# Batch 0's first products halved straight from PSUM by ScalarE and VectorE, with fewer state DMAs and a new order of the opening

## The chip, the cores and the metric

One core of a Trainium2 chip. The metric is the device time of one execution in microseconds, the median of three runs. The engines are TensorE (PE: matmuls; PEld: its weight loads), VectorE (DVE), ScalarE (ACT), GpSimd (POOL) and SyncE (SP), which issues most DMAs.

## What is computed

x is (8, 8, 512, 64), that is batches, heads, rows, width; state is (8, 8, 32, 64); w_ch1 is 512 x 2048, w_ch2 2048 x 512. Each batch is a two-way attention and then a feed-forward layer over the concatenated rows:

```python
s  = x @ state.T / 8;   a  = softmax(s);   xread = a @ state      # 512 rows per head
s2 = state @ x.T / 8;   a2 = softmax(s2);  sread = a2 @ x         # 32 rows per head
y  = concat([xread, sread]).transpose(0, 2, 1, 3).reshape(8, 544, 512)
yn = (y - mean) / sqrt(var + 1e-6) * g_ln
out = y + relu(yn @ w_ch1) @ w_ch2                                # (8, 544, 512), float32
```

## The kernel before

Every float32 product is made of three float16 products: both factors are split into a high half (the value rounded to float16) and a low half (the value minus its high half), and high x high, high x low and low x high are summed. A split so costs two instructions: ScalarE writes the high half, and another engine, mostly VectorE, subtracts it and writes the low half.

The first layer is not computed from xread. Per batch and unit u (the 2048 hidden columns are four units of 512) `state_products` (L656) multiplies the state with w1 (L662), which gives a small `matrix`; the hidden columns then are the softmax numerators `ea` times `matrix`: L705 in batch 0, L798 in the batches from 1 on. Behind that come relu, split, and the product with `w2h`, the split second weights: L719 in batch 0, L856 in the others, where the second layer goes by Strassen's scheme with the sums of weight blocks `sums`. The scores of a batch are made from transposes of x and state (`xT`, `sT`, two xT transposes per batch by DMA; L400), the second softmax's product is L474.

In the opening the weights arrive as raw words (`raw`, `sums` as buffers), are put together (`w_t`), w1 is weighted with g_ln and freed of its column means (L589, `acc`), the largest size is found (L598), and `w1c` and `w2h` are the scaled and split results, 128 x 2048 each per unit. ScalarE writes their high halves, VectorE the low ones. `x` is batch data split to float16, `x_f` the loaded one; `s_j`, `s_r` are loads of state, `sh`, `sk` its splits; `eb` numerators of the second softmax, `ef`, `ts` steps on the way to `ea`; `of_weights`, `uoq`, `hs` scales; `mv`, `rs`, `rf`, `of_unit` the layer norm's statistics; `part` the scaled second product of batch 0 on its way out; `z`, `sread` the second attention's result.

Batch 0's hidden tiles are made by `first_products` (L694 to L713): four units of four tiles of 128 x 512, each in one PSUM bank of the pool `acc` (four banks). `hidden` (L683) then takes three instructions: ScalarE's relu copies the bank into a strip in SBUF (three strips in turn), ScalarE copies the strip to the high half, GpSimd subtracts the high half from the strip. With `engine=nc.vector` nobody calls it before the change. In the batches from 1 on hidden tiles are split by other code, `strassen_hidden`.

Nothing of the order is left to a scheduler: every step is a closure made by `do` (so the profile shows L194 for all but matmuls), steps are gathered in streams (0 the gain, 1 the attention of batch 0, 2 to 5 the first weights, 6 state products, 7 first products, 8 to 11 the second weights, 17 to 20 the second products of batch 0 by unit, 25 and 26 attention and state products of batch 1, and so on, about 20 per batch), and the table `PLAN` names stream and step in the order of issue. Each engine runs its own instructions in that order, and a waiting instruction holds up all behind it on its engine; DMAs wait in the queue of the engine that issues them.

Of the kernel before, what the change touches and what calls it, by code (L numbers as in the profile page):

```python
# [10 lines left out]
F16 = mybir.dt.float16  # L11
# [157 lines left out]
WARM = 0  # L169


class Later:
# [36 lines left out]
def moe_attention(ctx: ExitStack, tc: tile.TileContext, x, state, g_ln, w1, w2, out):  # L209
# [27 lines left out]
    def rows(name):  # L237
        return block(8, "rows", 2, name)
# [742 lines left out]
```

## Time and profile before

| | us |
|---|---|
| median of 3 runs | 640.9 (640.69 to 643.12) |
| the profiled execution | 642.75 |
| its span | 641.0 |
| mean granted clock of TensorE | 0.971 |

The span is what the trace covers; 1.75 us of the execution lie around it. Shares and rows of the profile belong to the profiled execution. In rows of groups stand line, engine, operation, output <- inputs, their shapes, the count, then busy time and the mean ns of one, and behind the last bar the idle time of the engine ahead of them with what ended it. In the chain and the timeline stand the start and the length in us. DMA issues on the sync queue are marked SPq.

### The profile page before, as it was taken

How to read it: one execution, taken by the hardware profiler on the slowest of the kernel's cores; microseconds unless marked ns; L12 is line 12 of the kernel's file. 1: busy time of each engine (PE TensorE's matmuls, PEld its weight loads, DVE VectorE, ACT ScalarE, POOL GpSimd, SP SyncE). 2: the span in 40 equal slices, each digit the busy share in tenths (PEclk: the TensorE clock that was granted, in tenths of full speed). 3: DMA queues.
4: the chain of work that ended last, by engine and by line, in shares of the span. 5: the costliest groups of instructions: out<-in, count | busy, mean ns of one | idle time of the engine just before them, and what ended most of it. 6: DMA issues, size and time to landing. Idle time of an engine off the chain costs nothing.

```text
span 641.0 us, 15125 instructions
## 1 busy us (share of the span) xinstructions
PE 603.9 (94%) x6218; PEld 480.6 (75%) x6220; DVE 478.3 (75%) x954; ACT 369.1 (58%) x651; POOL 249.7 (39%) x213
## 2 busy tenths in 40 slices
PE   2769899899999999999999999999999999999996
PEld 1226556457978888888888778888888889898885
DVE  4999799778896779786976897677866878466344
ACT  4488999777564755644646553755465454344331
POOL 0013754387662324442532334234432443234122
PEclk9956799899999999999999999999999999999998
DMA  8985439523624243233631323304330404401002
GB/s 304 298 310 187 137 95 153 121 50 75 147 38 132 60 100 72 76 82 69 166 78 43 72 73 79 106 20 89 90 94 1 108 3 84 139 15 34 11 24 68
DMA packets 89382, 62.60 MB, mean 98 GB/s; under 512 B 67616, under 2 KB 81440, under 8 KB 88864
## 3 DMA queue, kind: packets, MB, share of 16 engines
q1 hardware_dynamic: 86512, 57.66, 34.3%
q0 software_dynamic: 864, 3.15, 2.6%
q8 instruction: 49, 0.80, 0.5%
q10 hardware_dynamic: 1936, 0.82, 0.5%
q14 instruction: 21, 0.17, 0.1%
HBM read 28.05 MB, written 9.44 MB: 58 GB/s over the span
## 4 chain that ended last, share of the span: by engine, by line
PE 83%; DVE 7%; ACT 5%; DMA 3%; issue 2%; ACTq 0%; SPq 0%; DVEq 0%
PE acc L856 42%; PE half L798 23%; PE acc L719 3%; PE half L808 3%; PE banks L662 3%; PE acc L705 3%; DVE w_t L194 2%; PE banks L474 2%; DMA xT<-x 1%; DMA sums<-in_moe_w_ch_dram 1%; PE banks L505 1%; PE banks L400 1%; PE acc L589 1%; ACT sums L194 1%; ACT raw L194 1%
## 5 line engine op out<-in xcount | busy, mean ns | idle before, releaser
L856 PEld LDWEIGHTS <-xs 128*128 128x128 f16 x2520 | 243.7, 98 | 36.4 <-issue 6.8
L194 POOL TENSOR_TENSOR xs<-rs,xs 128x512 f16<-128x512 f32 x120 | 139.8, 1179 | 234.9 <-ACT xs L194 154.3
L856 PE MATMUL acc<-w2h,xs 128*128 128x256 f16 x1440 | 181.1, 273 | 0.0
L798 PE MATMUL half<-ea,matrix 128*128 128x256 f16 x1344 | 160.9, 273 | 1.3 <-DVE rs L194 0.8
L798 PEld LDWEIGHTS <-matrix 128*128 128x128 f16 x1344 | 129.6, 98 | 21.6 <-issue 3.4
L856 PE MATMUL acc<-sums,xs 128*128 128x256 f16 x1080 | 141.8, 273 | 0.0
L194 DVE SCALAR_TENSOR_TENSOR rs<-half,rs 128x256 f32<-128x256 f32 x224 | 90.2, 416 | 48.5 <-ACT rs L194 25.4
L194 ACT ACTIVATE xs<-rs 128x512 f16<-128x512 f32 (+1 forms) x128 | 76.3, 618 | 55.0 <-DVE rs L194 47.7
L194 ACT ACTIVATE xs<-half 128x256 f16<-128x256 f32 (+1 forms) x112 | 52.9, 486 | 54.0 <-DVE rs L194 25.8
L194 DVE SCALAR_TENSOR_TENSOR xs<-half,xs 128x256 f16<-128x256 f32 (+1 forms) x112 | 60.9, 549 | 14.1 <-ACT xs L194 13.9
L194 ACT ACTIVATE rs<-half 128x256 f32<-128x256 f32 x56 | 21.2, 379 | 63.5 <-PE half L798 61.8
L719 PE MATMUL acc<-w2h,hid 128*128 128x512 f16 x192 | 43.0, 379 | 0.4 <-ACT part L194 0.4
L194 DVE SCALAR_TENSOR_TENSOR matrix<-banks,hs,matrix 128x1024 f16<-128x1024 f32 x28 | 35.6, 1273 | 9.6 <-ACT matrix L194 9.6
L194 DVE TENSOR_TENSOR strip<-acc,strip 128x256 f32<-128x256 f32 (+1 forms) x61 | 33.2, 544 | 6.5 <-ACT strip L194 3.0
L194 POOL TENSOR_TENSOR ts<-ts,mA 128x1024 f32<-128x1024 f32 (+1 forms) x8 | 14.4, 1805 | 53.8 <-DVE mA L194 44.0
L194 ACT ACTIVATE matrix<-banks,hs 128x1024 f16<-128x1024 f32 x28 | 31.0, 1109 | 7.1 <-PE banks L662 6.5
L719 PEld LDWEIGHTS <-hid 128*128 128x128 f16 x192 | 18.4, 98 | 22.2 <-issue 1.2
L705 PE MATMUL acc<-ea,matrix 128*128 128x256 f16 x192 | 29.0, 316 | 1.0 <-ACT xr L194 0.5
L194 POOL TENSOR_TENSOR hid<-strip,hid 128x512 f16<-128x512 f32 x16 | 21.3, 1342 | 19.5 <-ACT hid L194 19.5
L194 DVE SCALAR_TENSOR_TENSOR x<-x_f,x_s,x 128x512 f16<-128x512 f32 x32 | 25.3, 814 | 4.2 <-ACT x L194 4.1
L705 PEld LDWEIGHTS <-matrix 128*128 128x128 f16 x192 | 21.3, 113 | 8.4 <-issue 1.8
L589 PE MATMUL acc<-w_t,gm 128*128 128x512 f32 x32 | 19.3, 755 | 8.2 <-DVE w_t L194 8.2
(154 smaller groups left out, 752.1 us busy)
## 6 DMA issues: line engine op xcount, KB each, us to landing
raw<-in_moe_w_ch_dram SPq DMA_DIRECT2D x10, 1024.0 KB, 6.8
out_dram<-xr SPq DMA_DIRECT2D x16, 512.0 KB, 3.4
x_f<-in_x_dram SPq DMA_DIRECT2D x14, 512.0 KB, 5.5
sums<-in_moe_w_ch_dram SPq DMA_DIRECT2D x6, 1024.0 KB, 7.7
ek<-ea SPq DMA_DIRECT2D x56, 64.0 KB, 2.0
ek<-ek SPq DMA_DIRECT2D x7, 512.0 KB, 4.3
xr<-part POOLq DMA_DIRECT2D x6, 512.0 KB, 4.6
s_r<-in_state_dram SPq DMA_DIRECT2D x28, 64.0 KB, 2.4
```

The lines of the kernel that those rows point to most:

```text
L194: return lambda: f(*map(now, args), **{k: now(v) for k, v in kw.items()})
L400: nc.tensor.matmul(ps[32 * j:32 * j + 32, g, w * s:w * s + w], lhsT=sT[D * g:D * g + D, a, 32 * j:32 * j + 32], rhs=xT[D * g:D * g + D, k: ...
L474: nc.tensor.matmul(ps_z[:, j], lhsT=x16[:, a, i], rhs=ebT[:, k, :, c, 32 * j:32 * j + 32], start=c == 0 and n == 0, stop=c == C - 1 and n ...
L505: nc.tensor.matmul(px[:, c, D * h:D * h + D], lhsT=ek[:, h % 2, h // 2, (2 * t + c) * P:(2 * t + c + 1) * P], rhs=sk[:, h], start=True, st ...
L589: nc.tensor.matmul(ps, lhsT=gm[:, k:k + 1].broadcast_to([P, P]), rhs=t4[:, k], start=k == 0, stop=k == 3)
L662: nc.tensor.matmul((ps0, ps1)[g][32 * j:32 * j + 32], lhsT=sT[D * g:D * g + D, a, 32 * j:32 * j + 32], rhs=w[D * g:D * g + D, i, j], start ...
L705: nc.tensor.matmul(o[:, 256 * f:256 * f + 256], lhsT=m[:, g, i, P * (q + f):P * (q + f) + P], rhs=ea[:, s, k, g], start=f == 0 and g == 0 ...
L719: nc.tensor.matmul(po, lhsT=hid[:, i, q, c * P:(c + 1) * P], rhs=w[:, j, q], start=first and q == 0 and n == 0, stop=last and q == 3 and n ...
L798: nc.tensor.matmul(ps[:, 256 * q:256 * q + 256], lhsT=m[:, h, i, P * (2 * k + q):P * (2 * k + q) + P], rhs=ea[:, 0, j, h, 256 * g:256 * g ...
L808: nc.tensor.matmul(ps[:, 256 * q:256 * q + 256].rearrange("p (t n) -> p t n", t=2), lhsT=w[:, i, j, fs], rhs=xsT[:, :, 4 * a + j], start=q ...
L856: nc.tensor.matmul(po[o], lhsT=y[:, n, i, o] if o < 2 else x[:, o - 2, n, i], rhs=v[j], start=u == 0 and n == 0 and k == 0 and o in (2, 1, ...
```

## The change

Three pieces of code and the order.

`hidden` gets a direct form for `engine=nc.vector`: ScalarE writes the high half from PSUM, VectorE reads the bank again and writes max(p, 0) minus the high half. All 16 tiles of `first_products` use it, so stream 7 has 48 steps instead of 64.

```diff
     def hidden(ps, scale, hi, lo, n, engine=nc.vector):
+        if engine is nc.vector:
+            p = ps.rearrange("p (f t) -> p f t", f=n)
+            yield do(nc.scalar.activation, hi, p, AF.Relu)
+            yield do(nc.vector.scalar_tensor_tensor, lo, p, 0.0, hi, ALU.max, ALU.subtract)
+            return
         strips[0] += 1
...
-                    yield from hidden(ps, 1.0, *(h[:, i, q:q + 2, 256 * s:256 * s + 256] for i in range(2)), 2, nc.gpsimd)
+                    yield from hidden(ps, 1.0, *(h[:, i, q:q + 2, 256 * s:256 * s + 256] for i in range(2)), 2, nc.vector if DIRECT[4 * u + 2 * s + q // 2] else nc.gpsimd)
```

`DIRECT` is a tuple of 16 ones. The loads of `s_j` of the batches from 1 on are two DMAs instead of four, the store of a batch's `sread` rows is one instead of four, and `ek` is laid out with its two middle indices exchanged (as many DMAs as before):

```diff
+        if b == 0:
+            for j in range(4):
+                yield do(engines[j // 2].dma_start, out=sj[32 * j:32 * j + 32], in_=state[b, 2 * j:2 * j + 2].rearrange("g n d -> n g d"))
+        else:
+            for g in range(G):
+                yield do(nc.sync.dma_start, out=sj[:, g], in_=state[b].rearrange("(j g) n d -> g j n d", g=G)[g])
...
-            ek = rows("ek").bitcast(F16).rearrange("p (g j t) -> p g j t", g=G, j=4)
+            ek = rows("ek").bitcast(F16).rearrange("p (j g t) -> p j g t", g=G, j=4)
...
-        for j in range(4):
-            yield do(nc.sync.dma_start, out=sv[NS * b:NS * b + NS, j], in_=sread[32 * j:32 * j + 32])
+        yield do(nc.sync.dma_start, out=sread_rows[NS * b:NS * b + NS].rearrange("n (j e) -> j n e", j=4),
+                 in_=sread.rearrange("p g d -> p (g d)"))
```

`PLAN` is written anew up to the last second products of batch 1; behind that it is the same apart from the numbers of steps. A line of it, the beginning, before and after:

```diff
-    "0:0 1:1 1:6-7 1:5 1:0 1:2 1:9 1:3 0:2 1:4 0:5 1:12 1:8 1:10-11 1:13-15 0:3 1:16-19 4:0 4:2-3 4:1 2:0 1:79 1:26 "
+    "0:0 0:2 1:1 1:9 1:7 1:3 1:0 1:4 1:2 0:5-6 1:6 1:5 4:0 1:8 1:11 4:1 1:12 1:10 1:13-15 2:0 0:3 1:16 4:2-3 2:1 "
```

With the change all lines of the kernel move a little: `do` is L192 instead of L194, L705 becomes L711, L719 L725, L798 L804, L856 L862, L662 L663, L400 L402 and L589 L590.

On the engines the new order shows at three places. The names `of_weights`, `uoq` and `is` are scales of weights, `mv` and `s` statistics of row blocks, `x_t`, `x_m`, `x_i`, `x_s` the way to the scale of a batch's x.

The first is VectorE ahead of the low half of `w2h` of unit 0, the last row; the matmuls of L719 hang on that. Before:

```order
L194 SCALAR_TENSOR_TENSOR w1c<-w_t,of_weights,w1c 128x2048
L194 TENSOR_SCALAR uoq<-of_weights,is_298 128x1
L194 RECIPROCAL of_weights<-of_weights 128x1
L194 TENSOR_REDUCE x_t<-banks 2x1
L194 TENSOR_REDUCE of_weights<-acc 128x1
L194 TENSOR_SCALAR of_weights<-of_weights 128x1
L194 BN_AGGR mv<-s_736 128x2
L194 BN_STATS s_813<-xr 128x6
L194 SCALAR_TENSOR_TENSOR w2h<-w_t,of_weights,w2h 128x2048
```

And after:

```order
L192 SCALAR_TENSOR_TENSOR hid<-acc,hid 128x2x256
L192 TENSOR_SCALAR x_m<-banks 128x2
L192 BN_AGGR mv<-s_584 128x2
L192 SCALAR_TENSOR_TENSOR hid<-acc,hid 128x2x256
L192 TENSOR_SCALAR x_i<-x_m 128x2
L192 TENSOR_REDUCE of_weights<-acc 1x1
L192 SCALAR_TENSOR_TENSOR w1c<-w_t,of_weights,w1c 128x2048
L192 RECIPROCAL x_s<-x_i 128x2
L192 TENSOR_SCALAR of_weights<-acc 128x1
L192 SCALAR_TENSOR_TENSOR w2h<-w_t,of_weights,w2h 128x2048
```

Two of the new low halves of hidden tiles (`hid<-acc,hid`) have come in, four more stand further ahead; a BN_STATS of 128x512 and the reduce of 128x512 (`of_weights<-acc 128x1`) have moved behind.

The second place is the sync queue with the transposes of batch 0. Before:

```order
L194 DMA s_j<-in_state_dram 32x2x64
L575 DMA sums<-in_moe_w_ch_dram 128x2x1024 x2
L575 DMA raw<-in_moe_w_ch_dram 128x2x1024 x4
L575 DMA sums<-in_moe_w_ch_dram 128x2x1024
L194 DMA_TRANSPOSE xT<-x_108 128x16x128
L194 DMA_TRANSPOSE sT_198<-sh 128x2x128
L194 DMA_TRANSPOSE xT<-x_108 128x16x128
```

And after:

```order
L192 DMA s_j<-in_state_dram 32x2x64 x2
L576 DMA sums<-in_moe_w_ch_dram 128x2x1024 x2
L576 DMA raw<-in_moe_w_ch_dram 128x2x1024 x4
L192 DMA_TRANSPOSE xT<-x_108 128x16x128
L192 DMA_TRANSPOSE sT_167<-sh 128x2x128
L192 DMA_TRANSPOSE xT<-x_108 128x16x128
L576 DMA sums<-in_moe_w_ch_dram 128x2x1024
```

The third load into `sums` has moved behind the three transposes.

The third place is VectorE ahead of the low half of `ea` of batch 1, the last row; the first L798 hangs on that. Before:

```order
L194 SCALAR_TENSOR_TENSOR sums<-t_582,of_weights,sums 128x512
L194 TENSOR_REDUCE dA<-ts 128x32
L194 TENSOR_SCALAR dA<-dA 128x32
L194 RECIPROCAL dA<-dA 128x32
L194 SCALAR_TENSOR_TENSOR matrix<-banks,hs,matrix 128x2x512
L194 STREAM_TRANSPOSE ef<-ts 128x1024
L194 SCALAR_TENSOR_TENSOR xr<-acc,of_unit,xr 128x512
L194 SCALAR_TENSOR_TENSOR ea<-ef,ea 128x1024
```

And after:

```order
L192 SCALAR_TENSOR_TENSOR hid<-acc,hid 128x2x256
L192 SCALAR_TENSOR_TENSOR sums<-t_587,of_weights,sums 128x512
L192 TENSOR_REDUCE x_am<-s_j 128x1
L192 SCALAR_TENSOR_TENSOR sums<-t_654,of_weights,sums 128x512
L192 TENSOR_REDUCE dA<-ts 128x32
L192 TENSOR_SCALAR dA<-dA 128x32
L192 RECIPROCAL dA<-dA 128x32
L192 SCALAR_TENSOR_TENSOR sums<-t_587,of_weights,sums 128x512
L192 SCALAR_TENSOR_TENSOR xr<-acc,of_unit,xr 128x512
L192 STREAM_TRANSPOSE ef<-ts 128x1024
L192 SCALAR_TENSOR_TENSOR matrix<-banks,hs,matrix 128x2x512
L192 SCALAR_TENSOR_TENSOR ea<-ef,ea 128x1024
```

The fifteenth of the 16 new low halves (first row) now stands shortly ahead of ea's, the sixteenth behind it.

On TensorE, one group of 24 L662 of batch 0 (a unit's state products) stands behind the first matmuls of L719 instead of ahead of them, and 12 matmuls of L719 more stand behind the first L798 of batch 1; otherwise the matmuls between these two are as many as before.

More of the change, by code (lines that the diff above doesn't have):

```diff
@@ L41 @@
 PLAN = (
[127 rows of a table removed]
[124 rows of a table added]
 WARM = 0
+DIRECT = (1, 1, 1, 1, 1, 1, 1, 1, 1, 1, 1, 1, 1, 1, 1, 1)
 class Later:
@@ L295, in load_batch @@
                 yield do(engines[hh].dma_start, out=o, in_=i[:, :, 2 * hh:2 * hh + 2] if b == 0 else i)
-        for j in range(4):
-            yield do(engines[j // 2].dma_start, out=sj[32 * j:32 * j + 32], in_=state[b, 2 * j:2 * j + 2].rearrange("g n d -> n g d"))
+        if b == 0:
[4 more added lines that the diff above has]
+                yield do(nc.sync.dma_start, out=sj[:, g], in_=state[b].rearrange("(j g) n d -> g j n d", g=G)[g])
         for r in range(4 if b > 0 else 0):
@@ L488, in attention @@
         if b > 0:
-            ek = rows("ek").bitcast(F16).rearrange("p (g j t) -> p g j t", g=G, j=4)
+            ek = rows("ek").bitcast(F16).rearrange("p (j g t) -> p j g t", g=G, j=4)
             for i in range(2):
                 for j in range(4):
-                    yield do(nc.sync.dma_start, out=ek[32 * i:32 * i + 32, :, j], in_=ea[32 * j:32 * j + 32, 0, i])
+                    yield do(nc.sync.dma_start, out=ek[32 * i:32 * i + 32, j], in_=ea[32 * j:32 * j + 32, 0, i])
             yield do(nc.sync.dma_start, out=ek[64:128], in_=ek[0:64])
-        sv = sread_rows.rearrange("n (j g d) -> n j g d", g=G, j=4)
-        for j in range(4):
-            yield do(nc.sync.dma_start, out=sv[NS * b:NS * b + NS, j], in_=sread[32 * j:32 * j + 32])
+        yield do(nc.sync.dma_start, out=sread_rows[NS * b:NS * b + NS].rearrange("n (j e) -> j n e", j=4),
+                 in_=sread.rearrange("p g d -> p (g d)"))
         ux = column("ux")
@@ L505, in mix @@
                         nc.tensor.matmul(px[:, c, D * h:D * h + D],
-                                         lhsT=ek[:, h % 2, h // 2, (2 * t + c) * P:(2 * t + c + 1) * P],
+                                         lhsT=ek[:, h // 2, h % 2, (2 * t + c) * P:(2 * t + c + 1) * P],
                                          rhs=sk[:, h], start=True, stop=True, skip_group_check=True)
@@ L941, in moe_attention @@
     streams += [list(s) for s in products(B)]
-    warm = half()
     def warmth():
         for _ in range(WARM):
-            yield do(nc.tensor.matmul, warm, lhsT=ones, rhs=ones.unsqueeze(1).broadcast_to([P, 4, P]), start=True, stop=True)
+            yield do(nc.tensor.matmul, half(), lhsT=ones, rhs=ones.unsqueeze(1).broadcast_to([P, 4, P]), start=True, stop=True)
     streams.append(list(warmth()))
```

249 rows, old and new, of the table PLAN are left out of this document.

## The prediction

> **What bounds the kernel now.** I read the page first: the engines' shares, and TensorE's row and clock in the 40 slices of 16.0 us.
>
> ```profile
> span 641.0 us, 15125 instructions
> PE 603.9 (94%) x6218; PEld 480.6 (75%) x6220; DVE 478.3 (75%) x954; ACT 369.1 (58%) x651; POOL 249.7 (39%) x213
> PE   2769899899999999999999999999999999999996
> PEclk9956799899999999999999999999999999999998
> ```
>
> TensorE is the bound in all but the first eight slices, and what is weak behind the start is the eighth slice (112 to 128 us, clock 0.8). So I asked what TensorE waited for, over the whole span and then from 75 us on.
>
> ```profile
> PE banks L194 <- DVE x_am L194: 8.7, 1, 8.7
> PE acc L589 <- DVE w_t L194: 8.2, 5, 3.5
> ...
> PE banks L400 <- DMA xT<-x: 2.1, 1, 2.1
> PE half L798 <- DVE rs L194: 0.8, 1, 0.8
> PE half L798 <- DVE xs L194: 0.6, 1, 0.6
> PE acc L719 <- ACT part L194: 0.4, 1, 0.4
> ```
>
> The last four are all there is after 75 us. So a change of the opening can gain by an earlier start of L719 (batch 0's second products, from where TensorE always has work) and by the removal of the 2.1 us wait with what follows from it. The chain of waits shows what follows.
>
> ```profile
> 106.31 8.84 DMA xT<-x
> 115.19 1.48 PE banks L400 x17
> 116.67 2.31 PE acc L705 x12
> 118.98 5.18 PE acc L719 x24
> 124.16 1.31 PE acc L705 x12
> 125.47 0.77 PE banks L662 x24
> ```
>
> Behind the wait, L400's 24 matmuls of 64x512 take 1.48 us where L662's 24 of the same shape take 0.77, and L705 takes 2.31 where it takes 1.31 later: TensorE runs at about half rate for 3.8 us, which costs 0.71 + 1.00 = 1.71 us.
>
> Then the timeline, for the instructions that release TensorE at three places.
>
> ```profile
> 78.86 2.57 DVE L194 SCALAR_TENSOR_TENSOR w2h<-w_t,of_weights,w2h 128x2048 f16<-128x2048 f32 x1 [0.62 <-ACT w2h L194]
> 81.20 8.00 PE L719 MATMUL acc<-w2h,hid 128*128 128x512 f16 x36
> 104.06 0.73 DVE L194 SCALAR_TENSOR_TENSOR x<-x_f,x_s,x 128x512 f16<-128x512 f32 x1
> 138.03 2.33 DVE L194 SCALAR_TENSOR_TENSOR ea<-ef,ea 128x1024 f16<-128x1024 f32 x1 [0.55 <-ACT ea L194]
> 141.52 0.71 PE L798 MATMUL half<-ea,matrix 128*128 128x256 f16 x5
> ```
>
> L719 starts as VectorE's low half of w2h for unit 0 ends (81.4). L400 of batch 1 starts at 115.19, when xT has landed, 10.4 us after the last low half of batch 1's x (104.06 + 0.73 = 104.79). L798, the first product of batch 1, needs ea's low half, which ends at 140.36; TensorE came only at 141.52, so that one was ready in time. How busy the engines are between these points (columns: stretch, length, then busy time and count of PE, PEld, DVE, ACT, POOL):
>
> ```profile
> 12.30:81.50 69.20, 53.72 (x418) 29.09 (x421) 63.91 (x112) 54.42 (x76) 20.44 (x13) 0.78 0.74 241
> 81.50:92.30 10.80, 10.80 (x58) 5.44 (x57) 9.95 (x25) 10.80 (x14) 4.97 (x4) 1.00 0.28 99
> 92.30:140.40 48.10, 45.53 (x390) 24.71 (x389) 40.58 (x57) 38.83 (x59) 26.64 (x22) 0.96 0.60 114
> ```
>
> VectorE is busy 63.91 + 9.95 + 40.58 = 114.44 of 128.10 us, so 13.66 us of it are idle, 5.29 of them before L719. That is the room into which the change puts work.
>
> **The change part by part.** *Direct halving.* These rows are the groups of 40 to 150 us and, for VectorE, two neighbours of the timeline.
>
> ```profile
> L194 ACT ACTIVATE strip<-acc 128x512 f32<-128x512 f32 x16 | 9.4, 586 | 5.3 <-PE acc L705 5.1
> L194 ACT ACTIVATE hid<-strip 128x512 f16<-128x512 f32 x16 | 9.8, 623 | 0.1
> L194 POOL TENSOR_TENSOR hid<-strip,hid 128x512 f16<-128x512 f32 x16 | 21.3, 1342 | 19.5 <-ACT hid L194 19.5
> L194 ACT ACTIVATE matrix<-acc 128x512 f16<-128x512 f32 x8 | 4.4, 593 | 0.4 <-PE acc L662 0.4
> L194 DVE SCALAR_TENSOR_TENSOR matrix<-acc,matrix 128x512 f16<-128x512 f32 x8 | 5.4, 677 | 0.0
> 82.56 0.68 DVE L194 SCALAR_TENSOR_TENSOR matrix<-acc,matrix 128x512 f16<-128x512 f32 x1
> 83.15 0.23 DVE L194 TENSOR_SCALAR rs<-mv 128x2 f32<-128x2 f32 x2
> ```
>
> GpSimd loses 16 x 1342 ns = 21.3 us, ScalarE its 16 strips, 9.4 us; the new ScalarE high half from PSUM has the shape of matrix<-acc (593 ns against 623), so nothing there. VectorE gains 16 low halves with one operand in PSUM and one in SBUF, which is the shape of its matrix row: 677 ns in itself, 0.59 from its start to the next instruction's. I take 0.60 each, with 0.68 as the upper bound. Two meetings speak in VectorE's favour (two from the timeline of each engine, and a group for the undisturbed price):
>
> ```profile
> 92.15 1.65 DVE L194 SCALAR_TENSOR_TENSOR x<-x_f,x_s,x 128x512 f16<-128x512 f32 x1
> 90.11 3.15 POOL L194 TENSOR_TENSOR hid<-strip,hid 128x512 f16<-128x512 f32 x1 [5.10 <-ACT hid L194]
> 93.85 2.16 DVE L194 TENSOR_SCALAR sums<-sums 128x1024 uint32<-128x1024 uint32 x1
> 94.00 1.45 POOL L194 TENSOR_TENSOR hid<-strip,hid 128x512 f16<-128x512 f32 x1
> L194 DVE TENSOR_SCALAR raw<-raw 128x1024 uint32<-128x1024 uint32 x5 | 3.4, 680 | 0.0
> ```
>
> Beside GpSimd's hid an x low half takes 1.65 us instead of the 0.73 above, and a TENSOR_SCALAR 2.16 instead of 0.68. With hid gone from GpSimd I put the 0.9 of x back; the 1.5 of the other I leave out, as GpSimd's w_t and t operations may meet it instead: 2.4 us is the upper end. The Trainium skill, "SBUF — State Buffer", section "Who interferes with whom", says that a VectorE instruction with two SBUF inputs is held up by a GpSimd instruction that reads SBUF, and one with at most one SBUF input is not; the trace agrees for x (1.65 against 0.73), and no row of before shows the new low half. By that rule the new low half never meets GpSimd and the sum would stay as it is; without it, each meeting would add about 0.9.
>
> *Where it lies ahead of L719.* In VectorE's order (the first place shown above) six hid low halves now stand ahead of this w2h (the place shows the last two), 3.6 us, while one BN_STATS and one reduce of 128x512 moved behind it (some 1.2): +2.4 us of work into 5.29 us of idle time. If it all goes into the idle time, L719 starts where it did; that is my value. The ends: 12.3 + 63.91 + 2.4 = 78.6 without any wait, 2.8 us earlier; and 2.4 us later if none of it does. Each inserted low half waits for ScalarE's high half of the same tile, with w1c and w2h queued behind it on VectorE, and L719 behind those; that is what the upper end stands for.
>
> *TensorE's order.* One group of 24 L662 (unit 3's state products of batch 0) moves from ahead of the first L719, where TensorE idled, to behind it: +0.77 us.
>
> *The wait at L400.* Between the first L719 and batch 1's last x low half VectorE now has two more hid halves but one w1c low half (2.35 us at 100.07, below) and one low half of sums less (128x512 like x's, 0.73):
>
> ```profile
> 100.07 2.35 DVE L194 SCALAR_TENSOR_TENSOR w1c<-w_t,of_weights,w1c 128x2048 f16<-128x2048 f32 x1
> ```
>
> That is 1.2 - 2.35 - 0.73 = -1.9, and -0.9 for the freed x: the low half ends near 102.0, and xT lands 10.4 later, at 112.4. TensorE would come to L400 at 115.19 - 2.14 - 0.43 + 0.77 = 113.4 (the small wait for part goes with ScalarE's strips). So the wait goes, with 1.0 us to spare, and the half rate with it: -2.14 - 0.43 - 1.71 = -4.28 us. ScalarE, busy 10.80 of 10.80 us at 81.5 to 92.3, sets x's high halves; its 9.4 us less is the cover here. If xT stays late, all 4.28 stay.
>
> On the sync queue (the second place) batch 0's transposes move ahead of the third load of sums.
>
> ```profile
> 15.81 10.49 SPq L194 DMA_TRANSPOSE xT<-x  x1
> ```
>
> The first one sat 10.49 us in the queue; one load of seven fewer ahead of it frees batch 0's scores by one or two us, but the load of weights comes later by as much, and L719 hangs on VectorE's work, so I put 0.
>
> *ea of batch 1.* From 12.37 to ea's low half VectorE now has 15 more low halves (the last of them in the third place): 9.0, less 0.1 of trifles, 8.9 us. TensorE reaches L798 earlier: from 81.20 to 141.52 are 60.32 us; less 4.28, plus 0.77, less 2.62 for 12 of L719 (a half of the 5.18 above for 24) that now stand behind the first L798: 54.2, so at 135.4. VectorE: before's 140.36, with the 8.9 us filled into its 13.66 us of idle time, less the 0.9 from x, less the 2.7 that it waited for L400's result,
>
> ```profile
> L194 DVE TENSOR_REDUCE mB<-banks 128x2 f32<-128x1024 f32 x1 | 1.2, 1224 | 2.7 <-PE banks L400 2.7
> ```
>
> gives 136.8: TensorE waits 1.4 us there, a new stall. The waits of 0.75 and 0.59 us later (above, 0.8 and 0.6) left the clock as it was (9 in every slice of the page there) and the one of 2.14 did not; 1.4 is nearer to 0.75, so I add no half rate, and 1.7 us if it went as behind 2.14. "TensorE: Matmul & The Clock Gate", Part 1, in the Trainium skill puts the window after which an idle TensorE falls to half its clock at about 3.4 us; by it 1.4 us cost no half rate either and the sum is the same, but then the 2.14 should not have cost any, and there the trace differs. The ends: 12.3 + 114.44 + 8.9 - 2.4 = 133.2, without a wait and with both meetings recovered, gives no stall; 140.36 + 8.9 - 3.6 = 145.7, nothing filled, gives 10.3.
>
> *The rest.* A tile's bank of acc (four) is now held until VectorE's low half has read it, not ScalarE's strip, so L705 of the tile after next hangs on VectorE; priced within the two ends above. On GpSimd's queue the DMAs xr<-part, issued behind the hid subtractions, come earlier; nobody waits for them in the rows above, so 0. s_j from 4 to 2 DMAs per batch, sread_rows from 4 to 1, ek's other layout (56 DMAs as before): all on the sync queue, no wait of TensorE behind 75 us names one of them; 0, and if that cover were gone, tenths.
>
> **Sum.** -4.28 + 0.77 + 1.4 + 0 = -2.1 us. The profiled execution took 642.75 (span 641.0 and 1.75 around it), 1.85 above the median 640.9; the same terms give 640.65 there and 638.8 for the median. About 0.5%, 3.2 us, is what a measurement of this kernel can tell from no change.
>
> **The rivals.**
> *VectorE has waits to spare* (faster): the inserted halves also cure waits that were for hid and x, w2h ends earlier by 1.4 (half of the 2.8) and ea by 134.0, when TensorE then gets to L798: -4.28 + 0.77 - 1.4 = -4.9, 636.0. At the end w2h is at 78.6 and, with 0.6 more recovered than the two meetings, ea at 132.6: -6.3, 634.6. For it: 13.66 us idle, and 16 operations less on GpSimd. Against: VectorE would be busy nearly throughout.
> *VectorE becomes the bound* (slower): only half of the 8.9 us finds idle time, as each low half waits for its high half with the queue behind it. ea ends at 141.2, TensorE waits 5.8 at L798, with 1.71 of half rate: -3.5 + 5.8 + 1.7 = +4.0, 644.9. It turns slower than +3.2 from ea at 140.4, where it ended before. For it: 8.9 of 13.66 us is much to fill, and none of it may be idle before its tile is ready. With nothing filled, 145.7, it is +8.5.
> *xT stays late* (no change): the transposes of batch 1 start as late as before; the 4.28 stays, L798 comes later and finds ea ready; +0.77: 641.7, within 0.5%. Against: the 1.0 us to spare; for: it is little.
>
> **How the numbers follow.** Forecast 0.38, of which 0.12 lies below -3.2 (a smaller stall, an earlier w2h) and 0.26 within 0.5%; waits to spare 0.26; VectorE the bound 0.24; xT late 0.12. So faster 0.12 + 0.26 = 0.38, same 0.26 + 0.12 = 0.38, slower 0.24. The range goes from the lower end of the first rival, 634.5, to just past the half-filled case, 645.5; the rest beyond is the nothing-filled tail.
>
> **What would show it.** Right: no L400 wait for xT and clock 1.0 from 112 to 128 us; the first L725 (the old L719) at 81 us; a wait of 1 to 2 us at the first L804 (the old L798) for VectorE's ea; hid low halves of 0.68 us. Wrong: that wait at 5 us or more, an L725 start beyond 83 or before 79.5, xT landing after 113.4, or new waits of the second products for hid or for banks.

## The result, and the profile after

The changed kernel took 635.96 us (median of five runs, 635.85 to 637.95) against 640.69 for the kernel before: ratio 0.9937, 95% interval 0.9921 to 0.9953, that is 4.7 us or 0.6% to 0.7% faster. The forecast was 638.8 with a range of 634.5 to 645.5; the likeliest case gave 2.1 us of the 4.7, and the time is nearly that of the rival that gave 636.0, in which VectorE has waits to spare (its terms did not come as it had them, as shown further below). The span of the changed kernel's profiled execution is 633.3 us, with 2.66 us around it.

The page after, the same rows as before:

```profile
span 633.3 us, 15044 instructions
PE 596.7 (94%) x6218; PEld 477.1 (75%) x6220; DVE 482.5 (76%) x970; ACT 362.4 (57%) x635; POOL 224.0 (35%) x197
PE   2649899999999999999999999999999999999996
PEclk9958999999999999999999999999999999999999
```

TensorE still starts weakly, but its clock is full from the fifth slice on, without the dent at 112 to 128 us. What TensorE waits for behind 75 us:

```profile
PE half L804 <- DVE rs L192: 0.8, 1, 0.8
...
PE acc L725 <- DVE w2h L192: 0.4, 1, 0.4
```

The row left out is the 0.6 of before; one of 0.2 us for `xs` follows. The 2.1 us for xT have gone, and no wait for ea stands in their place. The timeline at the places of the prediction, first VectorE's first w_t, then the two ends of w2h (units 0 and 1), ea, and TensorE's three entries:

```profile
10.73 1.23 DVE L192 SCALAR_TENSOR_TENSOR w_t<-sums 128x1024 uint32<-128x1024 uint32 x1
74.51 2.33 DVE L192 SCALAR_TENSOR_TENSOR w2h<-w_t,of_weights,w2h 128x2048 f16<-128x2048 f32 x1
76.16 0.38 PE L725 MATMUL acc<-w2h,hid 128*128 128x512 f16 x1
86.14 2.35 DVE L192 SCALAR_TENSOR_TENSOR w2h<-sums,of_weights,w2h 128x2048 f16<-128x2048 f32 x1
107.58 1.04 PE L402 MATMUL banks<-xT,sT 64*32 64x512 f16 x24
128.95 1.23 DVE L192 SCALAR_TENSOR_TENSOR ea<-ef,ea 128x1024 f16<-128x1024 f32 x1
131.19 2.78 PE L804 MATMUL half<-ea,matrix 128*128 128x256 f16 x24
```

w2h of unit 0 ends at 76.84 instead of 81.43, and L725 starts at 76.16 instead of 81.20 (one matmul ahead of the 0.4 us wait above). VectorE between these points (columns as before; DVE is the third pair):

```profile
12.30:76.90 64.60, 46.37 (x394) 25.62 (x396) 63.65 (x114) 49.78 (x67) 9.67 (x8) 0.84 0.73 236
76.90:88.50 11.60, 11.60 (x95) 5.10 (x94) 11.54 (x27) 11.05 (x13) 2.47 (x3) 1.00 0.54 189
88.50:130.20 41.70, 41.70 (x341) 22.95 (x334) 39.92 (x65) 34.20 (x48) 13.79 (x11) 1.00 0.63 128
```

It is idle for 117.9 - 115.1 = 2.8 us in these 117.9, where before it was idle for 13.7 in 128.1: 1.0 us up to the first L725, 0.1 to unit 1's w2h, 1.8 to ea. The hidden tiles' groups:

```profile
L192 DVE SCALAR_TENSOR_TENSOR hid<-acc,hid 128x512 f16<-128x512 f32 x16 | 10.6, 676 | 0.3 <-ACT hid L192 0.2
L192 ACT ACTIVATE hid<-acc 128x512 f16<-128x512 f32 x16 | 9.4, 595 | 2.9 <-PE acc L711 2.9
```

These are the prices of the prediction (677 and 593), and VectorE waits 0.2 us in all for the high halves.

### The profile page after: what moved, and what is told of

It reads as the page before. It is cut to its first block, busy times and chain, and to the rows that moved or that the text cites. A ratio compares the mean times of both kernels' runs of the same rounds, so it can differ in the third digit from the quotient of the medians.

```text
span 633.3 us, 15044 instructions
## 1 busy us (share of the span) xinstructions
PE 596.7 (94%) x6218; PEld 477.1 (75%) x6220; DVE 482.5 (76%) x970; ACT 362.4 (57%) x635; POOL 224.0 (35%) x197
## 4 chain that ended last, share of the span: by engine, by line
PE 85%; DVE 8%; DMA 3%; ACT 2%; issue 1%; POOL 1%; SPq 0%; DVEq 0%; POOLq 0%; ACTq 0%
PE acc L862 42%; PE half L804 23%; PE acc L725 7%; PE half L814 3%; PE banks L663 3%; DVE w_t L192 2%; PE acc L711 2%; DMA x_f<-in_x_dram 2%; PE banks L476 2%; PE banks L506 1%; DMA sums<-in_moe_w_ch_dram 1%; PE banks L402 1%; DVE x L192 1%; PE banks L192 1%; DVE ts L192 0%
## 5 line engine op out<-in xcount | busy, mean ns | idle before, releaser
L862 PEld LDWEIGHTS <-xs 128*128 128x128 f16 x2520 | 243.6, 98 | 36.8 <-issue 6.8
L192 POOL TENSOR_TENSOR xs<-rs,xs 128x512 f16<-128x512 f32 x120 | 140.4, 1184 | 237.3 <-ACT xs L192 154.2
L862 PE MATMUL acc<-w2h,xs 128*128 128x256 f16 x1440 | 182.0, 273 | 0.2 <-POOL xs L192 0.2
L804 PE MATMUL half<-ea,matrix 128*128 128x256 f16 x1344 | 161.1, 273 | 1.3 <-DVE rs L192 0.8
L804 PEld LDWEIGHTS <-matrix 128*128 128x128 f16 x1344 | 129.6, 98 | 21.5 <-issue 3.4
L862 PE MATMUL acc<-sums,xs 128*128 128x256 f16 x1080 | 141.8, 273 | 0.0
L192 DVE SCALAR_TENSOR_TENSOR rs<-half,rs 128x256 f32<-128x256 f32 x224 | 90.0, 417 | 46.6 <-ACT rs L192 25.1
L192 ACT ACTIVATE xs<-rs 128x512 f16<-128x512 f32 (+1 forms) x128 | 76.4, 618 | 56.8 <-DVE rs L192 51.7
L192 ACT ACTIVATE xs<-half 128x256 f16<-128x256 f32 (+1 forms) x112 | 53.6, 486 | 62.4 <-DVE rs L192 24.9
L192 DVE SCALAR_TENSOR_TENSOR xs<-half,xs 128x256 f16<-128x256 f32 (+1 forms) x112 | 60.8, 549 | 19.5 <-ACT xs L192 17.1
L192 ACT ACTIVATE rs<-half 128x256 f32<-128x256 f32 x56 | 21.2, 378 | 53.2 <-PE half L804 51.3
L725 PE MATMUL acc<-w2h,hid 128*128 128x512 f16 x192 | 43.2, 379 | 0.4 <-DVE w2h L192 0.4
L192 DVE SCALAR_TENSOR_TENSOR matrix<-banks,hs,matrix 128x1024 f16<-128x1024 f32 x28 | 35.7, 1274 | 6.0 <-ACT matrix L192 5.9
L192 ACT ACTIVATE matrix<-banks,hs 128x1024 f16<-128x1024 f32 x28 | 31.1, 1109 | 14.2 <-PE banks L663 13.5
L192 DVE TENSOR_TENSOR strip<-acc,strip 128x256 f32<-128x256 f32 (+1 forms) x61 | 33.3, 546 | 6.7 <-PE acc L862 3.6
L725 PEld LDWEIGHTS <-hid 128*128 128x128 f16 x192 | 18.5, 98 | 22.1 <-issue 1.5
L192 POOL TENSOR_TENSOR ts<-ts,mA 128x1024 f32<-128x1024 f32 (+1 forms) x8 | 14.4, 1804 | 45.3 <-DVE mA L192 38.5
L192 DVE SCALAR_TENSOR_TENSOR x<-x_f,x_s,x 128x512 f16<-128x512 f32 x32 | 24.3, 787 | 4.3 <-ACT x L192 4.2
L711 PE MATMUL acc<-ea,matrix 128*128 128x256 f16 x192 | 23.5, 277 | 0.5 <-ACT xr L192 0.3
L663 PE MATMUL banks<-w1c,sT 64*32 64x512 f16 x672 | 23.6, 379 | 0.0
L192 ACT ACTIVATE x<-x_f,x_s 128x512 f16<-128x512 f32 x32 | 21.8, 715 | 3.0 <-DVE x_s L192 2.9
L192 DVE BATCH_NORM_STATS2 s<-xr 128x6 f32<-128x512 f32 x32 | 21.6, 680 | 1.6 <-ACT xr L192 1.6
```

Of the source, the lines that this page charges most:

```text
L192: return lambda: f(*map(now, args), **{k: now(v) for k, v in kw.items()})
L663: nc.tensor.matmul((ps0, ps1)[g][32 * j:32 * j + 32], lhsT=sT[D * g:D * g + D, a, 32 * j:32 * j + 32], rhs=w[D * g:D * g + D, i, j], start ...
L711: nc.tensor.matmul(o[:, 256 * f:256 * f + 256], lhsT=m[:, g, i, P * (q + f):P * (q + f) + P], rhs=ea[:, s, k, g], start=f == 0 and g == 0 ...
L725: nc.tensor.matmul(po, lhsT=hid[:, i, q, c * P:(c + 1) * P], rhs=w[:, j, q], start=first and q == 0 and n == 0, stop=last and q == 3 and n ...
L804: nc.tensor.matmul(ps[:, 256 * q:256 * q + 256], lhsT=m[:, h, i, P * (2 * k + q):P * (2 * k + q) + P], rhs=ea[:, 0, j, h, 256 * g:256 * g ...
L862: nc.tensor.matmul(po[o], lhsT=y[:, n, i, o] if o < 2 else x[:, o - 2, n, i], rhs=v[j], start=u == 0 and n == 0 and k == 0 and o in (2, 1, ...
```

## The experiments

The two theories at the start were these. A: the halving itself gains, as it takes GpSimd's collisions and ScalarE's copies away. B: the new order gains, and the halving alone only loads VectorE. Each kernel was timed against runs of the kernel before on the same chip, whose medians were 640.4 to 640.7 us. All change either the kernel before or the changed kernel in the one thing that their diff shows. The runs e2 and e3 take the change apart, e4 to e10 undo or load one piece of it, e11 and e12 ask whether the place of a load is a gain by itself. Differences to the changed kernel are given between medians; between the ratios they are up to 1.4 us smaller, and for e7, e8 and e9 they are 1.3 us each. The intervals of e4, e7, e8 and e9 overlap that of the changed kernel; what these runs show rests on their traces as well as on their times.

**e1, the kernel before again** (no edit).

> The kernel before, unchanged: a second trace and a null comparison. Ratio 1.000, 640.5 to 641.5 us. If the 2.1 us wait of L400 for xT and the half rate behind it belong to the kernel, they are here again within 0.5 us; if they were an accident of the first profiled execution (642.75 us against a median of 640.7), this trace has them smaller and is shorter by as much.

640.65 us, ratio 1.0006 (0.9993 to 1.0019). Its execution with a profile took 640.64, span 638.9. The rows are the clock in the 40 slices, the start of the second products, the wait at L400, and L798's entry:

```profile
PEclk9959799999999999999999999999999999999999
81.02 8.06 PE L719 MATMUL acc<-w2h,hid 128*128 128x512 f16 x36
114.61 0.84 PE L400 MATMUL banks<-xT,sT 64*32 64x512 f16 x24 [1.71 <-DMA xT<-x]
139.40 1.47 PE L798 MATMUL half<-ea,matrix 128*128 128x256 f16 x12
```

The wait for xT is there again, 1.71 us, but the 24 matmuls behind it take 0.84 us and not 1.48: the half rate was in the first of the two traces alone, and accounts for most of the 2.1 us by which that execution was longer. The clock has no dent at 112 to 128 us here, so its absence after the change is no gain of the change. e1's trace is therefore the one to set beside the changed kernel's: spans 638.9 and 633.3, 5.6 us.

**e2, the direct halving alone, in the old order.**

```diff
+        if engine is nc.gpsimd and n == 2:
+            p = ps.rearrange("p (f t) -> p f t", f=n)
+            def halves_now(hi, lo, p):
+                nc.scalar.activation(hi, p, AF.Relu)
+                nc.vector.scalar_tensor_tensor(lo, p, 0.0, hi, ALU.max, ALU.subtract)
+            yield do(halves_now, hi, lo, p)
+            for _ in range(2):
+                yield do(lambda: None)
+            return
```

> The kernel before with its own order and DMAs, and only the 16 hidden tiles halved directly (both halves at the place of the strip copy). Theory A, the halving itself frees VectorE from GpSimd's collisions (5.4 us of slowed instructions in before) and ScalarE from 16 copies: the first L719 starts 2 to 4 us earlier than 81.2, time 637 to 639. Theory B, the gain is the new order's and the halving alone only puts 9 us on VectorE: the first L719 at 81 to 84, ea of batch 1 ends after 141, time 641 to 645.

654.26 us, ratio 1.0196 (1.0170 to 1.0221): slower, and by more than either theory had. Of its five executions four took 651.85 to 655.33 us and one 2174.4, for which nothing on record gives a reason. VectorE's waits from 12 to 145 us, and where the second products got under way:

```profile
DVE hid L690 <- ACT hid L689: 8.0, 6, 3.2
...
89.67 5.52 PE L729 MATMUL acc<-w2h,hid 128*128 128x512 f16 x17 [2.26 <-DVE hid L690]
```

The low halves do not fall into VectorE's idle time. They wait 8.0 us for ScalarE's high halves, with everything behind them in VectorE's queue, and w2h of unit 0 ends at 88.0. This is the mechanism of the slower rival, in the old order. Both halves stand here at the first of the three old steps; a later step for the low half, which might wait less, was not tried.

**e3, the order alone, with the old halving** (`DIRECT` all zeros; the strip's two ScalarE copies at the step of the high half, GpSimd's low half at the step of VectorE's).

```diff
+        def both(ps, hi):
+            nc.scalar.activation(r, ps, AF.Relu, scale=scale)
+            nc.scalar.activation(hi, q, AF.Copy)
+        yield do(both, ps, hi)
```

> The changed kernel with its order and DMAs, but the 16 hidden tiles again over strip (ScalarE copies twice at the place of the high half) and GpSimd. Theory A: ScalarE's 9.4 us and the collisions come back, the first L725 starts 2 us or more later than 76.2, time 638.5 to 641. Theory B: the order keeps the gain and VectorE has 9 us less to do: first L725 at 76 or earlier, time 635 to 636.5.

644.79 us, ratio 1.0064 (1.0045 to 1.0083): slower than both kernels, so theory B falls; A had the direction, but its 638.5 to 641 was too little. The chain of what happened, TensorE's wait, VectorE's wait, and GpSimd's queue ahead of it:

```profile
PE banks L663 <- DVE ts L192: 5.3, 1, 5.3
...
120.28 0.87 DVE L192 SCALAR_TENSOR_TENSOR sums<-n,of_weights,sums 128x512 f16<-128x512 f32 x1 [5.66 <-ACT sums L192]
...
113.44 2.27 POOL L192 TENSOR_TENSOR hid<-strip,hid 128x512 f16<-128x512 f32 x2 [2.40 <-ACT hid L698]
...
117.11 1.15 POOL L192 TENSOR_TENSOR hid<-strip,hid 128x512 f16<-128x512 f32 x1 [0.18 <-ACT hid L698]
118.22 1.27 POOL L192 TENSOR_TENSOR n<-sums,t 128x512 f32<-128x512 f32 x1
```

n, a block sum of the second weights, stands behind hidden tiles that wait for ScalarE; the halves of n and then batch 1's scores (ts) are late on VectorE, and TensorE waits 5.3 us for a bank, with a granted clock of 0.50 in the 3.5 us behind that. Of these four kernels (before, e2, e3 and the changed one) only the one with both, order and halving, gains.

**e4, the state DMAs as before** (the loops of the diff's minus lines, in the changed kernel's steps).

> The changed kernel with the state loads and the sread stores as before (four DMAs each instead of two and one). Theories A and B: nobody waits for them, 636.0 within 0.5 us. A third theory, C, that fewer DMAs on the sync queue let xT land earlier: xT of batch 1 lands 1 us or more later and the time is 637 or more.

637.9 us, ratio 0.9946 (0.9925 to 0.9966). The median is 1.9 us above the changed kernel's, as theory C had it and A and B had not; between the ratios it is 0.6 us, and the six executions run from 635.39 to 638.79. In its trace the mechanism of C is missing: nobody on TensorE waits for xT behind 75 us, the first second product starts at 76.00 and batch 1's first product at 130.96, both 0.2 us earlier than in the changed kernel. Whether the fewer DMAs gain anything further on stays open.

**e5, strips back on ScalarE, low halves on VectorE.** GpSimd stays free.

```diff
-            yield do(nc.scalar.activation, hi, p, AF.Relu)
-            yield do(nc.vector.scalar_tensor_tensor, lo, p, 0.0, hi, ALU.max, ALU.subtract)
+        yield do(both, ps, hi)
+        r = q
+        yield do(engine.tensor_tensor, lo, r, hi, ALU.subtract)
```

> The changed kernel, but ScalarE copies the bank to the strip and the strip to the high half as before (16 more copies, 9.4 us), and VectorE takes the low half from the strip instead of PSUM. GpSimd stays free of the hidden tiles. Theory G, what the order needs is a GpSimd without the hidden tiles (in the run with the order alone its n operations came late behind them): within 1.5 us of the changed kernel, 636 to 637.5. Theory S, ScalarE's copies are what counts: 639 to 642, with ScalarE late at w2h's high halves.

644.39 us, ratio 1.0056 (1.0044 to 1.0068), above the ranges of both theories. Theory G falls: with GpSimd free of the hidden tiles it is as slow as e3. The low halves themselves, now with both operands in SBUF:

```profile
L192 DVE TENSOR_TENSOR hid<-strip,hid 128x512 f16<-128x512 f32 x16 | 16.4, 1038 | 1.5 <-ACT hid L693 1.5
```

The shortest takes 651 ns, but the mean is 1038, which makes 5.8 us more for the 16 than from PSUM. So two things were changed here, ScalarE's copies and the price of the low half; e10 takes ScalarE by itself.

**e10, each high half written twice by ScalarE, from PSUM.**

```diff
+            def twice(hi, p):
+                for _ in range(2):
+                    nc.scalar.activation(hi, p, AF.Relu)
+            yield do(twice, hi, p)
```

> The changed kernel with each of the 16 hidden high halves written twice by ScalarE, straight from PSUM: 16 x 0.5 us of ScalarE, but no strip and nothing more on VectorE or GpSimd. Theory S, what the order cannot bear is ScalarE's 8 to 9 us: 641 to 645, near the 644.4 of the run with strips. Rival, VectorE's low half from SBUF (its form with two SBUF inputs, or the strips' turn) made that run slow: 636.5 to 638.5 here.

640.38 us, ratio 0.9997 (0.9984 to 1.0010): between the two theories' ranges. ScalarE's 16 x 0.5 us cost 4.4 us against the changed kernel, by way of VectorE:

```profile
DVE hid L192 <- ACT hid L691: 3.5, 6, 1.0
...
134.34 1.23 DVE L192 SCALAR_TENSOR_TENSOR ea<-ef,ea 128x1024 f16<-128x1024 f32 x1
```

That is about half of e5's 8.4 us. The dearer low halves are the likely other half, which no run shows alone; in e5's trace a wait of 2.2 us for a bank, with a granted clock of 0.63 behind it, is part of that.

**e6, each low half written twice by VectorE.**

```diff
+            def twice(lo, p, hi):
+                for _ in range(2):
+                    nc.vector.scalar_tensor_tensor(lo, p, 0.0, hi, ALU.max, ALU.subtract)
+            yield do(twice, lo, p, hi)
```

> The changed kernel with each of the 16 hidden low halves written twice by VectorE: 16 x 0.6 us more of VectorE. Theory V, VectorE is the bound up to w2h of unit 1 (0.96 us idle up to unit 0's, 0.06 to unit 1's): the first L725 3.0 to 3.6 us later, unit 1's w2h 4.8 us later and TensorE waits there, ea of batch 1 some 9 us later with TensorE waiting at L804; time +7 to +10, 643 to 646. Rival, VectorE still has room: the first L725 under 1.5 us later, time below 639.

645.63 us, ratio 1.0087 (1.0071 to 1.0103), 9.7 us above the changed kernel, as theory V had it. w2h of units 0 and 1, ea, and the first product of batch 1:

```profile
78.00 2.33 DVE L192 SCALAR_TENSOR_TENSOR w2h<-w_t,of_weights,w2h 128x2048 f16<-128x2048 f32 x1
91.08 2.35 DVE L192 SCALAR_TENSOR_TENSOR w2h<-sums,of_weights,w2h 128x2048 f16<-128x2048 f32 x1
138.78 1.23 DVE L192 SCALAR_TENSOR_TENSOR ea<-ef,ea 128x1024 f16<-128x1024 f32 x1
140.21 2.78 PE L808 MATMUL half<-ea,matrix 128*128 128x256 f16 x24
```

They come 3.5, 4.9, 9.8 and 9.0 us later than in the changed kernel, for 3.6, 4.8 and 9.0 us of added work up to the two w2h and ea. TensorE waits not at the first product of batch 1, as theory V had it, but for hid (1.6 us) and for a bank (2.2). In the changed order, a microsecond of VectorE work added between its first w_t and ea is about one more of the kernel.

**e7, the third load of sums ahead of batch 0's transposes again.**

```diff
-... 4:7 3:1 4:8 ...  1:35 3:8 5:1 1:36 ...
+... 4:7 3:1 5:1 4:8 ...  1:35 3:8 1:36 ...
```

> The changed kernel with the third load of sums back ahead of batch 0's transposes on the sync queue, nothing else. Theory Q, the 1.6 to 2.0 us by which VectorE's first w_t starts earlier come from one load fewer beside the first ones: first w_t at 12.4 instead of 10.7, first L725 1.6 us later, 637.5 to 638. Rival, the first loads' order among x and state gives it: w_t stays at 10.7 to 11.1, time 636 within 0.5.

638.11 us, ratio 0.9957 (0.9942 to 0.9972), 2.1 us above the changed kernel's. Theory Q falls, since w_t starts at 10.70, and so does its rival, since L725 is late all the same. The transpose in the queue, then what VectorE waited for:

```profile
16.93 7.76 SPq L192 DMA_TRANSPOSE xT<-x  x1
33.50 0.78 DVE L192 STREAM_TRANSPOSE ts<-banks 128x256 f32<-128x256 f32 x2 [2.46 <-PE banks L402]
78.61 0.38 PE L725 MATMUL acc<-w2h,hid 128*128 128x512 f16 x1
```

In the changed kernel the first of these rows is this, and its ts has no wait:

```profile
16.98 5.23 SPq L192 DMA_TRANSPOSE xT<-x  x1
```

With one load more ahead of it, the transpose is 2.5 us longer in the queue, batch 0's scores are late, VectorE waits 2.5 us for them, and L725 starts 2.45 us later.

**e9, the very first DMAs in the order of before.**

```diff
-    "0:0 0:2 1:1 1:9 1:7 1:3 1:0 1:4 1:2 0:5-6 1:6 1:5 4:0 1:8 ...
+    "0:0 0:2 1:1 1:6-7 1:5 1:0 1:2 1:9 1:3 1:4 0:5-6 4:0 1:8 ...
```

> The changed kernel with the very first DMAs (x, state, gain) issued in the order of before on both queues, nothing else. Theory F, their order makes VectorE's first w_t start at 10.7 instead of 12.4 to 12.8: first w_t at 12 or later here, first L725 1.3 to 2 us later, 637.3 to 638. Rival, the later start in before has another cause: w_t stays at 10.7 to 11.1 and the time within 0.5 us of the changed kernel.

637.74 us, ratio 0.9957 (0.9940 to 0.9975), 1.8 us above the changed kernel. Theory F holds:

```profile
12.21 1.22 DVE L192 SCALAR_TENSOR_TENSOR w_t<-sums 128x1024 uint32<-128x1024 uint32 x1
...
77.83 0.38 PE L725 MATMUL acc<-w2h,hid 128*128 128x512 f16 x1
```

**e8, two of the six early tiles back on strip and GpSimd** (the form of e3 for these two).

```diff
-DIRECT = (1, 1, 1, 1, 1, 1, 1, 1, 1, 1, 1, 1, 1, 1, 1, 1)
+DIRECT = (1, 1, 1, 1, 0, 0) + (1,) * 10
```

> The changed kernel with two of the six tiles that are halved ahead of the first L725 (unit 1's first two, whose low halves stand right ahead of w2h on VectorE) back on strip and GpSimd. Theory V: VectorE's 1.2 us less lets L725 start 1 to 1.2 us earlier, unit 1's w2h too, time 634.8 to 635.4. Rival, GpSimd's two operations hold up VectorE or its own n operations: 636 to 638.

637.86 us, ratio 0.9957 (0.9946 to 0.9969), 1.9 us slower than the changed kernel: the rival. GpSimd's n, behind a hidden tile in its queue, now meets w2h's low half on VectorE:

```profile
72.36 3.55 POOL L192 TENSOR_TENSOR n<-w_t,t 128x512 f32<-128x512 f32 x1
74.81 3.25 DVE L192 SCALAR_TENSOR_TENSOR w2h<-w_t,of_weights,w2h 128x2048 f16<-128x2048 f32 x1
78.11 11.99 PE L728 MATMUL acc<-w2h,hid 128*128 128x512 f16 x47 [2.26 <-DVE w2h L192]
```

w2h takes 3.25 us instead of 2.33, and it starts 0.3 later though VectorE has two low halves less to do. It waits 0.5 us for TensorE (x_m), and the small x_i behind that meets GpSimd's t (71.01 to 72.28) and takes 1.16 us instead of 0.15:

```profile
71.15 1.16 DVE L192 TENSOR_SCALAR x_i<-x_m 128x2 int32<-128x2 int32 x1
```

TensorE then waits 2.26 us for w2h, and its 47 matmuls behind the wait take 11.99 us where the changed kernel's take 10.30 (granted clock 0.64 in the first 3.5 us). So the 1.9 us are not the price of slack: the two operations put back on GpSimd lengthen VectorE's own work by these two meetings, and the clock adds to it. What VectorE's slack by itself would be worth, no run shows.

**e11, one load more behind the transposes.**

```diff
-... 4:7 3:1 4:8 1:26 1:24 1:27 2:3 1:25 1:28 1:22 2:2 2:4-5 1:23 ...  3:7 1:33 1:35 ...
+... 4:7 4:8 1:26 1:24 1:27 2:3 1:25 1:28 1:22 1:23 1:33 3:1 2:2 2:4-5 ...  3:7 1:35 ...
```

> The changed kernel with one load more, the fourth raw, behind batch 0's transposes. If the transposes still wait for the loads ahead of them and VectorE for their scores, this is 1 to 2 us faster (634 to 635) and beats both kernels. If VectorE no longer waits for the scores (the changed kernel's trace names no such wait), nothing is gained and the words of the fourth load come late: 636 to 638.

641.85 us, ratio 1.0021 (1.0010 to 1.0033), 5.9 us slower than the changed kernel and above both expected ranges:

```profile
17.07 3.09 SPq L192 DMA_TRANSPOSE xT<-x  x1
...
DVE raw L192 <- DMA raw<-in_moe_w_ch_dram: 4.9, 1, 4.9
```

The transpose is 2.1 us shorter in the queue, and VectorE waits 4.9 us for the load that was put off.

**e12, the kernel before with the transposes first.**

```diff
-... 2:7 3:3 5:1 5:5 4:9 3:4 1:28 3:6 ...  3:12 1:23 4:11 1:33-34 ...
+... 2:7 3:3 1:28 1:23 1:33 5:1 5:5 4:9 3:4 3:6 ...  3:12 4:11 1:34 ...
```

> The kernel before with batch 0's three transposes moved ahead of the third load of sums on the sync queue, nothing else: the counterpart of the run that put the load back in the changed kernel (2.1 us slower there). Theory additive: 638 to 639. Rival, before has other waits behind which the earlier scores are hidden (VectorE waits for TensorE and ScalarE, not for L400 of batch 0): 640 to 641.

644.62 us, ratio 1.0059 (1.0043 to 1.0075): neither theory, it is 4 us slower than before.

```profile
15.83 7.95 SPq L194 DMA_TRANSPOSE xT<-x  x1
33.06 0.70 DVE L194 TENSOR_SCALAR sums<-sums 128x1024 uint32<-128x1024 uint32 x1 [3.89 <-DMA sums<-in_moe_w_ch_dram]
```

The old order has VectorE use the third load of sums early, and it waits 3.9 us for it. The same move of a load is worth 2.1 us in the new order, which has other work at that place, and costs 4 in the old.

None of the versions tried beats the changed kernel.

## Why the forecast was right, and where it was not

**Direction and range** were right; the likeliest case was not the one that came. Against e1's trace the 5.6 us of span are 4.86 for the earlier start of the second products (81.02 to 76.16) and 0.73 between them and batch 1's first product (58.38 us there before, 55.03 now, less the 2.62 for the 12 matmuls moved behind); behind that nothing changes. 0.9 us of it is lost again around the span (1.74 in e1, 2.66 after), for which no run gives a reason.

That the rival's 636.0 lies so near to 635.96 is luck in its terms: it had the second products start 1.4 us earlier and not 4.9, it took off 1.71 us of half rate that e1 does not have, and it had no loss around the span.

**"L719 starts where it did": this step failed.** It was put at 0, with 2.8 us earlier as the end, and it measured 4.9. The working began at VectorE's first w_t and held that fixed. But the first w_t itself starts 1.6 to 2.0 us earlier (10.73 against 12.37 and, in e1, 12.75), mostly through the order of the very first DMAs, which the prediction did not look at: with their old order w_t is 1.5 and L725 1.7 us later (e9). Here are e1's first w_t and its w2h of unit 0, and the engines' busy time from the first w_t to the end of that w2h in e1 and in the changed kernel (VectorE is the third pair):

```profile
12.75 1.23 DVE L194 SCALAR_TENSOR_TENSOR w_t<-sums 128x1024 uint32<-128x1024 uint32 x1 [0.38 <-ACT sums L194]
78.32 3.00 DVE L194 SCALAR_TENSOR_TENSOR w2h<-w_t,of_weights,w2h 128x2048 f16<-128x2048 f32 x1 [0.26 <-ACT w2h L194]
12.75:81.32 68.57, 51.99 (x419) 27.55 (x420) 64.36 (x110) 54.26 (x75) 22.12 (x14) 0.83 0.76 243
10.73:76.84 66.11, 46.65 (x393) 25.91 (x396) 65.16 (x116) 51.26 (x69) 9.67 (x8) 0.85 0.74 241
```

Against e1, w2h ends 4.5 us earlier: 2.0 by the earlier w_t and 3.3 by less idle time (4.2 to 0.95), less 0.8 of more work. The prediction had 2.4 more work there; part of the difference is w2h itself, which took 2.57 and 3.00 us in the two traces of before and takes 2.33 now.

**"On the sync queue ... I put 0": this failed too.** The reason given was that L719 hangs on VectorE's work. It does, but VectorE hangs on batch 0's scores, and these on the transposes: 2.45 us at L725, 2.1 in the time (e7). These 2.45 and e9's 1.7 are prices of single pieces with all others in place, and not shares of the 4.86: the old halving put back makes the same start 1.8 us later as well (77.96 in e3).

**The work fell into idle time,** as assumed. That this would happen was argued from the sum of idle time alone. e2 shows that it doesn't follow: the same 16 instructions in the old order wait 8.0 us for ScalarE. In that order they stood where their inputs were not ready yet; the new one puts them where they are, with 0.2 us of such waits.

**"TensorE waits 1.4 us" for ea: it did not.** ea ended at 130.18, 1.0 us before TensorE came. The term that was mis-sized is VectorE's work. From its first w_t to the end of ea, in e1 and in the changed kernel (in before it was busy for 114.4 of 128.0 us):

```profile
12.75:138.23 125.48, 106.80 (x864) 57.13 (x865) 115.03 (x189) 103.88 (x145) 53.76 (x38) 0.90 0.66 185
10.73:130.18 119.45, 99.93 (x820) 53.94 (x823) 116.65 (x206) 96.56 (x128) 25.92 (x22) 0.91 0.68 196
```

The prediction added 8.9 us of work and took off 0.9, for the one x low half; VectorE's busy time rose by only 1.6 to 2.2. Four meetings with GpSimd have gone, not one: the x low half (1.65 us before, 0.74 in the mean now) and the TENSOR_SCALAR of sums (2.16, now 0.67) beside GpSimd's hid, the four small of_unit (2.33 us in all before, 1.37 in e1, 0.88 now), and ea's own low half, whose 2.33 us the prediction took as given (1.23 now). It ran beside GpSimd's w_t, which the change does not remove but which now ends before ea. The w_t in before, and sums in the changed kernel:

```profile
136.65 2.63 POOL L194 TENSOR_TENSOR w_t<-w_t 128x512 f32<-128x512 f32 x2
L192 DVE TENSOR_SCALAR sums<-sums 128x1024 uint32<-128x1024 uint32 x1 | 0.7, 667 | 0.0
```

Together these are some 4 us (against e1) to 5 (against before), where the prediction took 0.9 and had 2.4 as the upper end.

**The wait at L400** went, as forecast, and the +0.77 for the moved group of L663 stands. But its 4.28 us held 1.71 of half rate that only one of the two traces of before has and that should not have been taken off a median; in e1 the waits that go are 1.71 and 0.39, about 2.1.

**The slower rival** had the right mechanism (e2, e6), and only the order decided against it. The rival that came had the right mechanism but the wrong cause: not fewer hidden tiles on GpSimd by themselves (e5 falls), but an order that rests on a ScalarE with 9.4 us less to do (e10), low halves from PSUM, and two moves in the DMA queues.

## What to carry to other kernels

Idle time of an engine is room for new work only where that work's inputs are ready and nothing urgent queues behind it: the halving cost 13.9 us in one order (654.26 against 640.38) and gained 8.8 in the other (644.79 to 635.96). When a table of issue order changes together with an operation, walk the first DMAs and the queue ahead of the first transposes too: in this case undoing either of two moves there made the point that set the end 1.7 and 2.5 us later. Before adding work to an engine, also price what its instructions now lose by running beside another engine's. And take a second profile before costing a loss that hangs on the clock.

## What was not expected of the hardware

- A low half from PSUM took 646 to 693 ns in all 16 cases of the changed kernel, 13 of them at least partly beside a tensor operation of GpSimd; the same low half with both operands in SBUF took 651 to 1785 (e5), and w2h's, with both operands in SBUF, 3.25 us beside GpSimd's n against 2.33 (e8). This agrees with the Trainium skill, "SBUF — State Buffer", section "Who interferes with whom", by which a VectorE instruction with at most one SBUF input, outside its two-port modes, does not contend with GpSimd. The prediction gave this rule without the words on the two-port modes, and its own TENSOR_SCALAR, with one SBUF input, took 2.16 us beside GpSimd's hid. e3 and e8 show such meetings from GpSimd's side as well: 3.30 us for a hid where 1.16 is usual, 3.55 for n where 1.27 is.
- The length of a wait does not by itself tell whether TensorE's clock falls. The mean granted clock in the 3.5 to 3.8 us behind a wait was 0.57 after 2.14 us (before), 0.52 and 0.64 after 2.26 (e2, e8) and 0.63 after 2.21 (e5), but 1.00 after 2.17 (e6), and 1.00 after 1.71 and 1.67 (e1, e12). What decides between 2.14 and 2.17, no run here tells.
